# Bias rows for two attention heads computed in place, and four loads moved to another queue

## The chip, the core and the metric

The kernel runs on one core of a Trainium2 chip. A core has a matrix engine (TensorE, PE in the profile), a vector engine (VectorE, DVE), a scalar engine (ScalarE, ACT), a general engine (GpSimd, POOL) and a sequencer that issues transfers (SyncE, SP). SBUF is on-chip memory of 128 partitions; PSUM, in 8 banks, takes what TensorE produces. SP and POOL issue DMA transfers, each into a queue of its own; the profile calls SP's "hardware_dynamic" (q1) and POOL's "software_dynamic" (q0). The metric is the device time of one execution in microseconds (us), the median of several runs.

## The reference

Attention over 8 batches of 8 heads (576 positions, 64 features each), with a bias that depends on a running sum of a gate `s`, and then a gated feed-forward block over all 4608 tokens.

```python
scores = (1/8) * q @ k.T
cum    = cumsum(maximum(s, 0))
bias   = -(cum[:, None] - cum[None, :])          # minimum with 0 under the causal mask
scores = where(causal, -1e9, scores + minimum(bias, 0))
attn   = softmax(scores)
x      = (attn @ v), heads side by side          # 4608 x 512
out    = (silu(x @ w_gate) * (x @ w_val)) @ w_out
```

Inputs and output are float32.

## The kernel before

The 64 heads are worked in 16 batches of four (`hb`, 0 to 15); heads 0 and 1 of a batch lie in one half of the 128 partitions, heads 2 and 3 in the other. For a batch, k and q are loaded as float32 (`load_one`), cast to bf16 (`cast_one`, or `cast_half` for half a batch), transposed so that the features lie on partitions, and copied out of PSUM into `KQ[hb % 2][r]` (`pe_out`), r being the pair of heads: partitions 64r to 64r+63 hold the features. The other 64 partitions of the tile are zero but for the rows that carry the bias. One matmul over all 128 partitions then gives the product and the bias together.

The bias needs the running sum split into two bf16 parts, a high and a low one. `HL` holds, for each of the 64 heads, four rows for the q side and four for the k side (`HL[:, row, side, :]`, with side 0 for q): the two parts, and constants 1 and -1 that pair with them. VectorE fills it: two clears with constants (L200, L201), the scale of s (L226), the scan (L227), the high part (L230), the low part (L231) and a copy to the other side (L232). `aug(hb, engs)` (L178) then sends, per head, four rows of 2 x 576 values into the tile with one DMA; for batches 0 to 3 by SP, later by POOL.

`score_piece(bh, ci)` computes one of four chunks of a head: a mask matmul where the chunk lies on the diagonal, the score matmuls (L359), and the exponential by ScalarE (L369) straight from PSUM into `pt`. `av_piece` (L396) multiplies with V, whose rows are cast into `VT` by `cast_v` (L168) after `load_v` (L157), five pieces c = 0 to 4 of a batch; V 0 is the V of the first eight heads. The result is transposed (`x_pe`) into `XT`, and the feed-forward part (L629, L650 and following) works on 512 tokens at a time while later heads are slipped in between its steps (`attn_items`).

The order of the work is written out by hand: each engine executes its instructions in the order in which the program emits them, and the waits follow from the data. The change touches the beginning alone, up to the scores of batch 1 (heads 4 to 7). There `keep_warm(n)` puts n small matmuls whose result nobody reads on TensorE; `row_half` transposes half a batch and copies it out; `half_batch` does batch 1; `scores(h)` is the four chunks of head h. SP issues s, the four halves of k 0 and q 0, the rows of batches 0 to 3, then V 1 and k, q of batches 4 and 5. POOL issues k, q of batch 1, V 0 (five pieces), the gate weights (`w_load`, L332), and k, q of batches 2 and 3 between the casts of V 0.

Of the kernel before, what the change touches and what calls it, by code (L numbers as in the profile page):

```python
# [19 lines left out]
def kernel(  # L20
# [20 lines left out]
    HB = 4  # L41
# [56 lines left out]
    HL = const.tile([BH, 4, 2, S], BF16)  # L98
# [6 lines left out]
    s_sb = first.tile([BH, S], FP32)  # L105
    c8 = first.tile([BH, S], FP32)
# [3 lines left out]
    with tc.manual_schedule():  # L110
# [67 lines left out]
        def aug(hb, engs):  # L178
            for hh in range(HB):
# [8 lines left out]
        nc.sync.dma_start(s_sb, s.rearrange("b h n -> (b h) n"))  # L188
# [4 lines left out]
        for r in range(NR):  # L193
            load_one(0, "k", (r, r + 1))
            load_one(0, "q", (r, r + 1))

# [3 lines left out]
        nc.vector.memset(HL[:, 0:2, 0, :].bitcast(FP32), ONES2)  # L200
        nc.vector.memset(HL[:, 2:4, 1, :].bitcast(FP32), NEGS2)  # L201
# [5 lines left out]
        )  # L207

        def pads(i):
            for r in range(2):  # L210
                nc.gpsimd.memset(KQ[i][r][64 * r : 64 * r + 64, :, NR * S :], 0.0)  # L211

        for r in range(2):
            nc.gpsimd.memset(aug_rows(0, r)[:, 1, :], 0.0)
            nc.scalar.mul(
                KQ[0][r][64 * (1 - r) : 64 * (1 - r) + 64, 0, :],
                one_s[0:64, 0:1].to_broadcast([64, NR * S + 64]), 0.0,
            )
        pads(0)
        nc.vector.memset(aug_rows(1, 0), 0.0)  # L220
        for nm in ("k", "q"):
            load_one(1, nm, eng=nc.gpsimd)
        init_vt(0)
        pads(1)

        nc.vector.tensor_scalar(s_sb, s_sb, 0.0, 8.0, ALU.max, ALU.mult)  # L226
        nc.vector.tensor_tensor_scan(  # L227
            c8, one_s[0:BH, 0:1].to_broadcast([BH, S]), s_sb, 0.0, ALU.mult, ALU.add
        )
        nc.vector.tensor_copy(HL[:, 0, 1, :], c8)  # L230
        nc.vector.tensor_sub(HL[:, 1, 1, :], c8, HL[:, 0, 1, :])  # L231
        nc.vector.tensor_copy(HL[:, 2:4, 0, :], HL[:, 0:2, 1, :])  # L232
# [652 lines left out]
        def row_half(nm, r, eng):  # L885
            for g in range(2):
                pe_transpose_half(0, nm, g, r)
            for g in range(2):
                pe_out(0, nm, g, r, eng)
# [6 lines left out]
        def scores(h):  # L896
            for ci in range(4):
                score_piece(h, ci)
# [6 lines left out]
        keep_warm(32)  # L905
        cast_half(0, "k", 0, nc.scalar)
        cast_half(0, "q", 0, nc.scalar)
        aug(0, SP4)
        row_half("k", 0, nc.scalar)
        row_half("q", 0, nc.vector)  # L910
        cast_half(0, "k", 1, nc.scalar)
        cast_half(0, "q", 1, nc.gpsimd)
        nc.gpsimd.memset(aug_rows(1, 1), 0.0)
# [151 lines left out]
```

## Time and profile before

| | us |
|---|---|
| median of 3 runs | 377.03 (375.74 to 377.14) |
| profiled execution, its time | 375.79 |
| its span | 374.0 |
| TensorE busy | 360.7 (96%) |
| VectorE busy | 289.6 (77%) |
| ScalarE busy | 240.4 (64%) |
| POOL busy | 212.3 (57%) |
| first score matmul starts | 10.91 |
| first exponential starts | 11.34 |
| first feed-forward matmul starts | 25.80 |

The granted TensorE clock was 0.999 of full speed. The busy time of an engine counts its instructions alone, not the issuing of transfers by SP or POOL, which the views in order of time list as DMA_DIRECT2D with the time for which the issuing engine was held. A transfer's landing is later than its issue; for POOL's queue the profile gives the time from the one to the other. An engine that idles costs time only where the work that ends last runs through it.

### The profile page before, as it was taken

The page shows a single profiled execution, that of the slowest core. Times are in us where ns is not written, and L with a number is a line of the kernel's source. Part 1 is how long each engine was busy: PE and PEld are TensorE (multiplying, and loading weights), DVE is VectorE, ACT ScalarE, POOL GpSimd, SP SyncE. Part 2 cuts the span into 40 slices and gives each one's busy share as a digit, 9 for nine tenths or more (in the row PEclk, how much of TensorE's full clock was granted, in tenths as well). Part 3 has the DMA queues.
Part 4 walks back from the last instruction along what each step waited for, and adds up shares of the span by engine and source line. Part 5 has one row for each costly group of instructions (what it writes and reads, how often), then busy time and mean ns, then how long its engine had stood idle before and what let it go on. Part 6 is the DMA issues. An engine that isn't in the chain of part 4 may idle for free.

```text
span 374.0 us, 8759 instructions
## 1 busy us (share of the span) xinstructions
PE 360.7 (96%) x3259; PEld 230.6 (62%) x3300; DVE 289.6 (77%) x578; ACT 240.4 (64%) x471; POOL 212.3 (57%) x325
## 2 busy tenths in 40 slices
PE   7799899999999999999999999999999999999995
PEld 6584456655555556855685559655865585476464
DVE  8968776468995899588967997699858867975984
ACT  8777677698876877588757875686566523323321
POOL 8883555856455647494649464955675516315320
PEclk9999999999999999999999999999999999999999
DMA  7899999799877997896779675984132103002003
GB/s 239 193 258 253 219 257 267 237 303 247 245 186 220 254 262 196 178 281 205 211 167 266 178 182 174 255 206 98 40 119 62 35 19 128 2 0 95 20 0 114
DMA packets 97146, 64.23 MB, mean 172 GB/s; under 512 B 77232, under 2 KB 82736, under 8 KB 97104
## 3 DMA queue, kind: packets, MB, share of 16 engines
q1 hardware_dynamic: 84976, 41.46, 45.2%
q0 software_dynamic: 12128, 22.21, 22.6%
q8 instruction: 26, 0.43, 0.5%
q14 instruction: 16, 0.13, 0.1%
HBM read 37.90 MB, written 19.86 MB: 154 GB/s over the span
## 4 chain that ended last, share of the span: by engine, by line
PE 85%; DMA 6%; POOL 5%; ACT 1%; issue 1%; DVE 1%; DVEq 0%; POOLq 0%; ACTq 0%
PE bank L629 45%; PE bank L735 17%; PE bank L359 10%; PE bank L396 7%; PE bank L686 5%; DMA rawk<-in_k_dram 4%; DMA rawv<-in_v_dram 2%; POOL rawv L157 1%; POOL vt L168 1%; POOL wv L332 1%; ACT pt L369 1%; PE bank L287 0%; POOL rawq L140 0%; ACT kq L314 0%; POOL kq L211 0%
## 5 line engine op out<-in xcount | busy, mean ns | idle before, releaser
L369 ACT ACTIVATE pt<-bank 128x512 bf16<-128x512 f32 (+1 forms) x256 | 120.4, 510 | 31.0 <-PE bank L359 18.2
L629 PE MATMUL bank<-XT,wg 128*128 128x512 bf16 x418 | 110.3, 379 | 1.2 <-DVE pp L652 0.3
L629 PE MATMUL bank<-XT,wv 128*128 128x512 bf16 x412 | 109.3, 379 | 1.1
L650 ACT ACTIVATE th<-bank 128x512 bf16<-128x512 f32 x108 | 64.7, 599 | 55.9 <-PE bank L629 53.6
L652 DVE SCALAR_TENSOR_TENSOR pp<-th,bank 128x512 bf16<-128x512 bf16 x108 | 73.6, 682 | 19.2 <-ACT th L650 18.7
L663 DVE SCALAR_TENSOR_TENSOR ht<-pp,bank 128x512 bf16<-128x512 bf16 x108 | 74.1, 686 | 10.6 <-PE bank L629 0.4
L359 PE MATMUL bank<-kq 128*128 128x128 bf16 (+4 forms) x576 | 75.6, 240 | 1.5 <-DMA kq<-HL 1.0
L672 POOL TENSOR_TENSOR ht<-ht 128x512 bf16<-128x512 bf16 x35 | 40.4, 1154 | 52.2 <-DVE su L670 52.1
L359 PEld LDWEIGHTS <-kq 128*128 128x128 bf16 x576 | 45.8, 98 | 31.5 <-issue 1.9
L629 PEld LDWEIGHTS <-wv 128*128 128x128 bf16 x432 | 38.4, 98 | 36.5 <-issue 0.6
L629 PEld LDWEIGHTS <-wg 128*128 128x128 bf16 x432 | 38.3, 98 | 34.2 <-issue 0.7
L396 PEld LDWEIGHTS <-pt 128*128 128x128 bf16 x960 | 41.9, 98 | 17.2
L374 POOL TENSOR_SCALAR_AFFINE_SELECT pt<-pt 128x512 bf16<-128x512 bf16 x56 | 36.8, 658 | 27.3 <-ACT pt L369 22.7
L396 PE MATMUL bank<-vt,pt 128*128 128x65 bf16 x960 | 47.0, 194 | 0.4 <-POOL vt L168 0.3
L430 POOL DMA_DIRECT2D xs<-ot x24 | 21.7, 905 | 30.0 <-DVE ot L413 27.6
L735 PEld LDWEIGHTS <-ht 128*128 128x128 bf16 x336 | 31.2, 98 | 4.3
L413 DVE TENSOR_TENSOR ot<-bank,rc 128x320 bf16<-128x320 f32 x64 | 31.5, 492 | 2.2
L183 POOL DMA_DIRECT2D kq<-HL x48 | 28.9, 604 | 0.0
L735 PEld LDWEIGHTS <-su 128*128 128x128 bf16 x252 | 23.5, 98 | 3.3
L686 PE MATMUL bank<-wo,ht 128*128 128x512 bf16 x90 | 24.8, 379 | 0.3
L800 POOL TENSOR_TENSOR ysb<-ysb 128x512 f32<-128x512 f32 x12 | 15.2, 1270 | 15.3 <-DVE ysb L794 15.3
L379 POOL TENSOR_SCALAR_AFFINE_SELECT pt<-pt 128x64 bf16<-128x64 bf16 x56 | 14.8, 264 | 15.8 <-ACT pt L369 15.7
(93 smaller groups left out, 384.6 us busy)
## 6 DMA issues: line engine op xcount, KB each, us to landing
out_dram<-ysb POOLq DMA_DIRECT2D x32, 256.0 KB, 4.5
rawv<-in_v_dram SPq DMA_DIRECT2D x28, 256.0 KB
rawk<-in_k_dram SPq DMA_DIRECT2D x12, 576.0 KB
rawq<-in_q_dram SPq DMA_DIRECT2D x12, 576.0 KB
xs<-ot POOLq DMA_DIRECT2D x24, 160.0 KB, 3.5
ks<-ck SPq DMA_DIRECT2D x11, 288.0 KB
qs<-cq SPq DMA_DIRECT2D x11, 288.0 KB
rawk<-in_k_dram POOLq DMA_DIRECT2D x3, 576.0 KB, 7.3
```

Of the source, the lines that this page charges most:

```text
L359: nc.tensor.matmul(sc[:, o : o + w], T[:, 1, e * S + 128 * tj : e * S + 128 * (tj + 1)], T[:, 0, e * S + lo : e * S + hi], start=not maske ...
L369: nc.scalar.activation(pt[:, c0 : c0 + n], sc, AF.Exp, scale=0.125)
L374: nc.gpsimd.affine_select(pt[:, 1088:1600], pt[:, 1088:1600], pattern=[[0, 4], [1, 128]], compare_op=ALU.is_ge, fill=zreg, base=0, channel ...
L396: nc.tensor.matmul(av[:, bi * (D + 1) : (bi + 1) * (D + 1)], pt[:, c0 : c0 + 128], VT[b % 2][:, tj, h, :], start=(tj == 0), stop=(tj == bi),)
L413: nc.vector.tensor_mul(ot[:, :, e * D : (e + 1) * D], av3[:, :, 0:D], rc[:, :, None].to_broadcast([128, NCH, D]),)
L629: nc.tensor.matmul(view(bs, TT), w[:, c, f0 : f0 + 128], xt[:, c, :], start=(c == 0), stop=(c == 3),)
L650: nc.scalar.activation(th, pg, AF.Tanh, scale=0.5)
L652: nc.vector.scalar_tensor_tensor(pp, in0=th, scalar=1.0, in1=pg, op0=ALU.add, op1=ALU.mult)
L663: nc.vector.scalar_tensor_tensor(hp[:, 2 * k2 : 2 * k2 + 2, :].rearrange("p a n -> p (a n)"), in0=pp, scalar=0.5, in1=pv, op0=ALU.mult, op ...
L672: (nc.vector if ft == NFT - 1 else nc.gpsimd).tensor_sub(hp[:, 1:3, :], hp[:, 1:4:2, :], hp[:, 0:3:2, :])
L686: nc.tensor.matmul(view(pys[ts_], DM), hps[ft // 2][:, 2 * (ft % 2) + half, c0 : c0 + 128], WO[j][:, ft % WKO, :], start=(ft == 0), stop=( ...
L735: nc.tensor.matmul(ps, lhs(p), rhs(p), start=(first and p == 0), stop=(last and p == NP - 1), skip_group_check=True,)
```

## The change

It has four parts. First, heads 0 and 1 no longer get their rows by DMA. s is loaded a second time, as 32 rows (partitions 64 to 95, sixteen copies of heads 0 and 1 in turn), so the scale, scan and split run on 96 partitions instead of 64. Masks made from columns of the identity matrix (`roles`, `a_q`, `a_k`, `b_lo`) say which row is a high part, a low part or a constant, and `sums_rows(e)` writes the 32 rows of the q side and of the k side of head e into `KQ[0][0]` with two VectorE operations, four for both heads. These heads use eight rows instead of four; 32 rows of the tile are cleared again before batch 2 uses it. Second, the clears of the tiles are spread differently over ScalarE, VectorE and POOL. Third, SP issues k 1, q 1 and piece 0 of V 0, which POOL issued before. Fourth, the written order changes: the cast of the second half of k 0 goes to POOL and that of q 0 to ScalarE; batch 1's casts go from VectorE to POOL; the copies out of PSUM are dealt differently; the scores of head 0 come ahead of the transposes of the second q half; batch 1's transposes move one head later; the warming matmuls are 38, 6 and 12 instead of 32, 10 and 10.

```diff
-    HL = const.tile([BH, 4, 2, S], BF16)
+    HL = const.tile([96, 4, 2, S], BF16)
...
-    s_sb = first.tile([BH, S], FP32)
-    c8 = first.tile([BH, S], FP32)
+    s_sb = first.tile([96, S], FP32)
+    c8 = first.tile([96, S], FP32)
+    roles = first.tile([96, 4], FP32)
...
-        nc.sync.dma_start(s_sb, s.rearrange("b h n -> (b h) n"))
+        s_rows = s.rearrange("b h n -> (b h) n")
+        nc.sync.dma_start(s_sb[64:96, :], s_rows[None, 0:2, :].to_broadcast([16, 2, S]))
+        nc.sync.dma_start(s_sb[0:64, :], s_rows)
...
             load_one(0, "q", (r, r + 1))
+        load_qk(1)
...
-        nc.vector.memset(HL[:, 0:2, 0, :].bitcast(FP32), ONES2)
-        nc.vector.memset(HL[:, 2:4, 1, :].bitcast(FP32), NEGS2)
+        up = slice(64, 96)
+        for rows in (KQ[0][1][0:64, :, :], KQ[0][0][96:128, :, :]):
+            n = rows.shape[0]
+            nc.scalar.mul(
+                rows.rearrange("p a n -> p (a n)").bitcast(FP32),
+                one_s[0:n, 0:1].to_broadcast([n, NR * S + 64]), 0.0,
+            )
+        nc.vector.memset(aug_rows(1, 0), 0.0)
...
-        for r in range(2):
-            nc.gpsimd.memset(aug_rows(0, r)[:, 1, :], 0.0)
-            nc.scalar.mul(
-                KQ[0][r][64 * (1 - r) : 64 * (1 - r) + 64, 0, :],
-                one_s[0:64, 0:1].to_broadcast([64, NR * S + 64]), 0.0,
-            )
-        pads(0)
-        nc.vector.memset(aug_rows(1, 0), 0.0)
-        for nm in ("k", "q"):
-            load_one(1, nm, eng=nc.gpsimd)
         init_vt(0)
-        pads(1)
+
+        nc.vector.tensor_add(roles[up], ident[up, 64:68], ident[up, 68:72])
+        nc.vector.tensor_reduce(
+            a_q[up], roles[up, 0:2], axis=mybir.AxisListType.X, op=ALU.add, negate=True
+        )
+        nc.vector.tensor_add(a_k[up], roles[up, 2:3], roles[up, 3:4])
+        nc.vector.memset(b_lo, -1.0)
+        nc.vector.tensor_reduce(b_lo[up], ident[up, 64:68], axis=mybir.AxisListType.X, op=ALU.add)
+        nc.vector.tensor_scalar_add(b_lo[up], b_lo[up], -1.0)
+        nc.vector.memset(HL[0:64, 0:2, 0, :].bitcast(FP32), ONES2)
+        nc.vector.memset(HL[0:64, 2:4, 1, :].bitcast(FP32), NEGS2)
...
-        nc.vector.tensor_sub(HL[:, 1, 1, :], c8, HL[:, 0, 1, :])
-        nc.vector.tensor_copy(HL[:, 2:4, 0, :], HL[:, 0:2, 1, :])
+        nc.vector.scalar_tensor_tensor(
+            HL[:, 1, 1, :], in0=HL[:, 0, 1, :], scalar=b_lo, in1=c8,
+            op0=ALU.mult, op1=ALU.add,
+        )
+
+        def sums_rows(e):
+            for side, a, m in ((1, a_k, e), (0, a_q, 2 + e)):
+                nc.vector.tensor_scalar(
+                    KQ[0][0][up, side, e * S : (e + 1) * S],
+                    HL[up, 1, 1, :], a[up, :], roles[up, m : m + 1],
+                    ALU.mult, ALU.add,
+                )
...
-        keep_warm(32)
+        keep_warm(38)
         cast_half(0, "k", 0, nc.scalar)
         cast_half(0, "q", 0, nc.scalar)
-        aug(0, SP4)
-        row_half("k", 0, nc.scalar)
-        row_half("q", 0, nc.vector)
-        cast_half(0, "k", 1, nc.scalar)
-        cast_half(0, "q", 1, nc.gpsimd)
-        nc.gpsimd.memset(aug_rows(1, 1), 0.0)
-        load_v(0, range(5), nc.gpsimd)
+        load_v(0, range(1))
+        row_half("k", 0)
+        row_out("k", 0, nc.scalar, nc.scalar)
+        row_half("q", 0)
+        keep_warm(6)
+        cast_half(0, "k", 1, nc.gpsimd)
+        load_v(0, range(1, 5), nc.gpsimd)
+        sums_rows(0)
+        row_out("q", 0, nc.scalar, nc.vector)
+        row_half("k", 1)
+        cast_half(0, "q", 1, nc.scalar)
+        nc.vector.tensor_copy(HL[0:64, 2:4, 0, :], HL[0:64, 0:2, 1, :])
+        aug(0, SP4, (2, 3))
+        aug(1, SP4)
+        sums_rows(1)
         w_load("g", 0)
-        aug(1, SP4)
-        keep_warm(10)
-        row_half("k", 1, nc.scalar)
-        row_half("q", 1, nc.vector)
-        keep_warm(10)
-        cast_one(1, "k", nc.vector)
-        cast_one(1, "q", nc.vector)
+        cast_one(1, "k", nc.gpsimd)
+        cast_one(1, "q", nc.gpsimd)
+        keep_warm(12)
+        scores(0)
+        row_half("q", 1)
+        row_out("k", 1, nc.vector, nc.vector)
+        row_out("q", 1, nc.vector, nc.vector)
         for c in range(3):
             cast_v(0, c, nc.gpsimd)
         load_one(2, "k", eng=nc.gpsimd)
...
-        scores(0)
+        scores(1)
         half_batch("k")
-        scores(1)
+        score_piece(2, 0)
+        score_piece(2, 1)
         half_batch("q")
-        scores(2)
+        score_piece(2, 2)
+        score_piece(2, 3)
         scores(3)
...
         cast_v(0, 4, nc.vector)
+        nc.gpsimd.memset(KQ[0][0][up, 1, 0 : NR * S].bitcast(FP32), 0.0)
         aug(2, SP4)
```

More of the change, by code (lines that the diff above doesn't have):

```diff
@@ L104 @@
     first = first_sbuf.enter_context(tc.tile_pool(name="first", bufs=1))
-    s_sb = first.tile([BH, S], FP32)
-    c8 = first.tile([BH, S], FP32)
+    s_sb = first.tile([96, S], FP32)
+    c8 = first.tile([96, S], FP32)
+    roles = first.tile([96, 4], FP32)
+    a_q = first.tile([96, 1], FP32)
+    a_k = first.tile([96, 1], FP32)
+    b_lo = first.tile([96, 1], FP32)
     PTP = {0: first, "bufs": 7}
@@ L176, in aug_rows, with aug @@
             return KQ[i][r][r0 : r0 + 64, :, :].bitcast(FP32)
-        def aug(hb, engs):
-            for hh in range(HB):
+        def aug(hb, engs, hhs=range(HB)):
+            for hh in hhs:
                 r, e = divmod(hh, 2)
@@ L207 @@
         )
-        def pads(i):
-            for r in range(2):
-                nc.gpsimd.memset(KQ[i][r][64 * r : 64 * r + 64, :, NR * S :], 0.0)
+        nc.gpsimd.memset(aug_rows(1, 1), 0.0)
+        nc.gpsimd.memset(KQ[0][0][0:96, :, NR * S :], 0.0)
+        nc.gpsimd.memset(KQ[0][1][64:128, :, NR * S :], 0.0)
         for r in range(2):
-            nc.gpsimd.memset(aug_rows(0, r)[:, 1, :], 0.0)
-            nc.scalar.mul(
-                KQ[0][r][64 * (1 - r) : 64 * (1 - r) + 64, 0, :],
-                one_s[0:64, 0:1].to_broadcast([64, NR * S + 64]), 0.0,
-            )
@@ L219 @@
-        pads(0)
-        nc.vector.memset(aug_rows(1, 0), 0.0)
-        for nm in ("k", "q"):
-            load_one(1, nm, eng=nc.gpsimd)
-        init_vt(0)
-        pads(1)
+            nc.gpsimd.memset(KQ[1][r][64 * r : 64 * r + 64, :, NR * S :], 0.0)
+        init_vt(0)
+        nc.vector.tensor_add(roles[up], ident[up, 64:68], ident[up, 68:72])
[3 more added lines that the diff above has]
+        nc.vector.tensor_add(a_k[up], roles[up, 2:3], roles[up, 3:4])
@@ L226 @@
+        nc.vector.memset(b_lo, -1.0)
[3 more added lines that the diff above has]
+        nc.vector.memset(HL[0:64, 2:4, 1, :].bitcast(FP32), NEGS2)
         nc.vector.tensor_scalar(s_sb, s_sb, 0.0, 8.0, ALU.max, ALU.mult)
         nc.vector.tensor_tensor_scan(
-            c8, one_s[0:BH, 0:1].to_broadcast([BH, S]), s_sb, 0.0, ALU.mult, ALU.add
+            c8, one_s[0:96, 0:1].to_broadcast([96, S]), s_sb, 0.0, ALU.mult, ALU.add
@@ L883, in keep_warm, with row_half, row_out @@
                 nc.tensor.matmul(view(spare, 128), ident, ident, start=True, stop=True)
-        def row_half(nm, r, eng):
+        def row_half(nm, r):
             for g in range(2):
                 pe_transpose_half(0, nm, g, r)
+        def row_out(nm, r, *engs):
             for g in range(2):
-                pe_out(0, nm, g, r, eng)
+                pe_out(0, nm, g, r, engs[g])
         def half_batch(nm):
```

## The prediction

> **What bounds the kernel now.** I read the page first (busy times, the chain that ended last), then the first 45 us by stages and in order of time, because every edit lies in the first 20 us. The page says that from about 40 us on the kernel is TensorE work end to end:
>
> ```profile
> PE 360.7 (96%) x3259; PEld 230.6 (62%) x3300; DVE 289.6 (77%) x578; ACT 240.4 (64%) x471; POOL 212.3 (57%) x325
> ...
> PE   7799899999999999999999999999999999999995
> ...
> PE 85%; DMA 6%; POOL 5%; ACT 1%; issue 1%; DVE 1%; DVEq 0%; POOLq 0%; ACTq 0%
> ```
>
> So a microsecond gained or lost before the feed-forward part starts (25.8 us) reaches the end, except where a later stall absorbs it. What sets that start is seen in the order of time (start, length, engine, line; in brackets the idle time before it):
>
> ```profile
> 4.21 1.35 DVE L227 TENSOR_TENSOR_SCAN c<-one_s,s_sb 64x576 f32<-64x576 f32 x1
> ...
> 6.08 0.75 DVE L231 TENSOR_TENSOR HL<-c,HL 64x576 bf16<-64x576 f32 x1
> ...
> 7.51 16.73 SPq L183 DMA_DIRECT2D kq<-HL  x16
> ...
> 9.51 4.89 POOL L157 DMA_DIRECT2D rawv<-in_v_dram  x5
> ...
> 10.91 0.83 PE L359 MATMUL bank<-kq 128*128 128x128 bf16 x8 [0.99 <-DMA kq<-HL]
> ...
> 11.34 13.53 ACT L369 ACTIVATE pt<-bank 128x512 bf16<-128x512 f32 x32 [1.63 <-PE bank L359]
> ```
>
> The first scores wait for the bias rows' DMA, 3.4 us after its issue at 7.51. Then 32 exponentials run on ScalarE without a gap from 11.34 to 24.87, 0.423 us each: this stage is ScalarE's, and its end lets the feed-forward part begin. One more stall of TensorE is large, and the chain that ended last passes through it (start, length, what):
>
> ```profile
> 22.81 15.78 DMA rawk<-in_k_dram
> ...
> 38.72 1.15 POOL ck L246
> ...
> 39.92 0.45 PE bank L287 x5
> ```
>
> TensorE idles 1.16 us there until k of batch 3 has landed and been cast. In the DMA stages (busy time of each engine, granted clock, DMA share, GB/s) two holes show, where POOL's k, q 1 start late and where they have ended before V arrives:
>
> ```profile
> 6.00:7.00 1.00, 1.00 (x17) 0.86 (x16) 0.93 (x3) 1.00 (x2) 0.90 (x3) 1.00 1.04 157
> ...
> 9.00:10.00 1.00, 0.92 (x15) 0.71 (x13) 0.93 (x2) 0.71 (x2) 1.00 (x2) 1.00 0.94 383
> 10.00:11.00 1.00, 0.09 (x2) 0.10 (x3) 0.97 (x2) 0.00 (x0) 1.00 (x2) 1.00 0.24 81
> ```
>
> **Step 1, the first exponential.** VectorE, from 1.06: clear of KQ[1] 1.1; six tiny operations for the masks at 0.06 (the 128x1 clear) to 0.19 (the 128x5 reciprocal), 0.4 to 1.2, say 0.8; the two HL clears 1.2 (start to start); scale, scan, cast and low half 3.25, the scan's 96 rows costing what 64 do. That ends at 7.4, as now. The two row operations for head 0 are new: 32x576 in bf16, bounded by half of the 64x1152 copy (0.27) and by the 0.55 of the float one; 0.45 each, by the 576-wide cast at 0.45: 8.3. One q copy, 0.72: 9.0. ScalarE: one more issue on SP (0.59) stands before k 0, so its cast starts by 5.3 instead of 4.69; casts 1.3, three copies of 0.7, the first 0.55 after the k cast as now: 8.6. TensorE: the second k half, cast on POOL (0.66 after a landing near 6.9, 0.6 later than the packets show now): 7.55; it also waits for ScalarE's k copies (7.9), transposes 0.69, twelve warming matmuls at 0.073: 9.5. The last is latest, so the first exponential is at 9.5 + 0.43 = 9.9, 1.4 us earlier. The clears moved between ScalarE, POOL and VectorE lie beside the loads until 4.7 and cost nothing there; were that cover gone, 0.37 to 1.1 each.
>
> **Step 2, head 2.** Heads 0 and 1 end at 9.9 + 8 x 0.423 = 13.3. Two things must then be there; now head 2 starts its exponentials at 14.7.
> (a) The transposes of batch 1's k now stand ahead of head 2 on TensorE, and their cast moves from VectorE (0.76 and 1.12) to POOL, behind V's issues. POOL: 7.55, three issues at 1.05 and the half one at 0.69 (from the 4.89), wg 0.78, cast 1.14: 13.3. Transposes 0.67 and 0.65 to the first exponential: 14.6, level with now. The early start is spent here.
> (b) Its bias rows still come by SP's queue, and there the change puts 1.15 MB of k, q 1 and the first 256 KB of V ahead of them. SP's queue is served in order: the k load issued at 43.39 moves its first packet at 49.0, when the V pieces before it end. And V pieces on SP starve beside POOL's traffic:
>
> ```profile
> 24.54 18.74 SPq L157 DMA_DIRECT2D rawv<-in_v_dram  x5
> ```
>
> Five issues held SP 18.7 us. From 29 to 34 us the packets alternate one for one, some 190 of V's 256 bytes each and 190 of the weights' 768 bytes per us; alone, at 44 us, V made 800. The moved piece has 64 packets per DMA engine. k, q 1 end near 10.5 (7.5, and 512 packets at 173 per us). From 9.6 POOL's queue holds V's other parts (14 packets per engine, 0.2 to 0.27 us each) and from 13.5 wg 0 (32 per engine, about 0.12 us). If the two queues alternate throughout, the piece ends with wg 0, at 18.3. By the issue row (18.74 us for 4.5 such pieces, 4.2 each) it ends at 15; alone it would take 1.3 us: 12. I take 17.5, near the alternation, which is the same pair of queues at packet level, less some turns in gaps before wg 0. Rows of head 2 then land at 17.6, its exponentials start at 18.2, and the remaining 24 need 10.15: 28.4. ScalarE's stage ends 3.5 us later; both ends kept: -0.1 (a alone) and +4.3.
>
> **Step 3, behind it.** POOL casts the moved piece first of V, so k 2, q 2 and five loads behind it are issued 1 to 2.5 us later (k 3 at 24 to 25 instead of 22.81). The transfers before them are done by 18 instead of 22.9 (wg 0's issue at 14.39 plus 8.5), so k 3 lands within 1 us of now, while TensorE asks for it 3.5 us later: the 1.16 us stall goes, -1.2. In case (a) alone k 3 is ahead by 1 to 3 us and the stall goes too. Next late would be the stalls of 32 to 36 us (0.8 in all, VectorE and ScalarE pacing), which stay.
>
> [...]
>
> **Costed at nothing.** ScalarE's half cast of q (0.67) lies before the first exponential; VectorE's four more copies (1.36 moved from ScalarE, 1.46 kept) end before 14, beside heads 0 and 1, and without that cover cost 0.7 each. The eight copies for batch 1 end at about 20 instead of 18.0, when the late heads still need them no earlier. The clear of 32 rows on POOL (0.55) sits after k 3's issue, where POOL idles 1.36 us; but the SP issue for batch 2's head 0 waits for it, and behind that stand seven row issues and V 1.
>
> **Sum.** +3.5 - 1.2 = +2.3 on the profiled execution (span 374.0, time 375.79, 1.8 outside): 378.1. The median of the runs is 377.03, 1.24 above that execution, so the forecast is 379.3, slower; its own range is 377.6 (piece at 15.5) to 380.6.
>
> **Rivals.**
> A, the piece finds gaps. If it has its 64 turns before wg 0's packets begin, it lands by 14 and (a) decides: -0.1 - 1.2 = -1.3, 375.7, not slower. The point is that: V's parts leaving some 1 us of gap per engine between 10.5 and 13.5. For it: POOL's issues are 1.05 apart and four packets take 0.8 at best. Against it: V's packets now take 0.27 on average, and bias rows sent beside them land 3 to 5 us after their issue.
> B, V 1 slips as well. SP's row issues for batch 2 wait for POOL's clear, V 1 is issued near 29 instead of 24.54 and lands up to 3 us after the 49 of now; its last cast is asked for from 52.5. Price 0 to 2 over the forecast: 381.
> C, ScalarE never stalls: casts and rows of head 2 by 13. The full 1.4 and the 1.2 come: 374.4. Against it: POOL's sum in (a).
>
> **How the numbers follow.** Forecast 0.48, A 0.27, B 0.10, C 0.15. A measurement of this kernel tells about 0.5% (1.9 us) from no change. Faster: C and a little of A, 0.16. Within: most of A and the part of the forecast with the piece before 17, 0.39. Slower: the rest of the forecast and B, 0.45. The range goes from near C (374.6) to B (381.2).
>
> **What would show it.** Step 1: first exponential near 9.9. Step 2: a ScalarE gap after the eighth, ended by the DMA of the bias rows (forecast) or by the batch 1 cast (A), and none in C; V's first cast on POOL waiting for its DMA. Step 3: no TensorE wait on k 3's cast near 40 us. I am wrong if the moved piece lands by 14, or if TensorE after 30 us makes up the late start.

## The result, and the profile after

The changed kernel takes 380.40 us (median of 7 runs, 377.97 to 382.33) where the kernel before takes 375.88 (7 runs, 375.46 to 377.19): ratio 1.0111, 95% interval 1.0074 to 1.0148. It is slower by 4.2 us by that ratio and by 4.5 between the two medians; the forecast was 379.3, which was 2.3 above the 377.03 that the median of before's first three runs was. The profiled execution took 377.97 (span 376.0) against 375.79 (374.0) before, which is +2.2 where the sum of the forecast said +2.3. One thing has to be known to read the rest: executions of the changed kernel differ more than those of before, and its profiled one is the fastest of its seven, so a second trace of it was taken (below).

In order of time, the lines of the changed kernel that answer to those shown of before (start, length, engine, line; in brackets the idle time before and what ended it):

```profile
8.50 3.54 POOL L161 DMA_DIRECT2D rawv<-in_v_dram  x4
...
9.84 0.91 DVE L943 COPY HL<-HL 64x1152 bf16<-64x1152 bf16 x1
...
10.55 1.69 ACT L391 ACTIVATE pt<-bank 128x512 bf16<-128x512 f32 x4 [0.28 <-PE bank L381]
...
10.83 19.14 SPq L187 DMA_DIRECT2D kq<-HL  x14
...
11.40 1.53 DVE L250 TENSOR_SCALAR kq<-HL,a_q,roles 32x576 bf16<-32x576 bf16 x1
...
13.41 1.69 ACT L391 ACTIVATE pt<-bank 128x512 bf16<-128x512 f32 x4 [1.16 <-PE bank L381]
...
17.22 0.62 PE L381 MATMUL bank<-kq 128*128 128x128 bf16 x6 [1.00 <-DMA kq<-HL]
...
17.65 8.43 ACT L391 ACTIVATE pt<-bank 128x512 bf16<-128x512 f32 x20 [2.55 <-PE bank L381]
...
28.91 0.59 PE L651 MATMUL bank<-XT,wg 128*128 128x512 bf16 x2
```

Read it from the top. The first exponential starts at 10.55 instead of 11.34: the rows written by VectorE are worth 0.8 us. Then ScalarE stops twice, 1.16 us before head 1 and 2.55 us before head 2 (13.41 and 17.65), where it ran without a gap before. Head 1 waits because the second of its row operations (11.40) took 1.53 us, not 0.42; head 2 waits for its bias rows, which SP issued only at 10.83 and which TensorE gets at 17.2. The feed-forward part starts at 28.91 instead of 25.80, 3.1 later. One thing is given back. From 30 to 40 us TensorE is busy for 9.18 us of 10, where it was 8.02 before: the stall for k of batch 3 is gone (the kernel before, then the changed one; columns: the stretch, its us, then busy us and instructions of PE, PEld, which are the weight loads of TensorE, DVE, ACT, POOL, the granted clock, the DMA share, GB/s):

```profile
30.00:40.00 10.00, 8.02 (x50) 4.02 (x50) 8.64 (x13) 7.22 (x14) 2.93 (x5) 1.00 1.20 259
...
30.00:40.00 10.00, 9.18 (x67) 5.14 (x67) 8.26 (x13) 7.80 (x14) 1.53 (x4) 1.00 1.21 262
```

The best single view is how late each kernel is against before at the same activation of the feed-forward part (ScalarE's `th`, 108 of them; start in the trace minus start in the trace of before, in us). It shows at once which losses last and which are absorbed:

| kernel | 1st, 30 us | after the k 3 stall, 41 us | after V 1, 57 us | 120 us | 159 us | last, 360 us |
|---|---|---|---|---|---|---|
| changed kernel | +3.11 | +1.77 | +1.78 | +1.98 | +1.98 | +2.13 |
| the same, second trace (e8) | +1.26 | -0.08 | +1.72 | +2.52 | +3.88 | +4.00 |
| e1 | +1.66 | +0.33 | +0.33 | +0.33 | +0.33 | +1.40 |
| e2 | +3.47 | +2.14 | +2.15 | +2.15 | +3.51 | +3.76 |
| e3 | +2.46 | +1.12 | +4.92 | +5.33 | +6.68 | +6.85 |
| e4 | +4.72 | +3.38 | +3.38 | +3.38 | +3.39 | +3.38 |
| e5 | +2.80 | +1.47 | +3.38 | +3.38 | +3.39 | +3.41 |
| e6 | +2.96 | +1.63 | +1.64 | +1.64 | +3.01 | +3.17 |
| e7 | +3.15 | +1.82 | +1.82 | +1.82 | +3.44 | +3.47 |
| e9 | +6.75 | +5.42 | +5.41 | +5.41 | +6.75 | +6.91 |
| e10 | +1.05 | -0.29 | -0.29 | -0.28 | -0.28 | -0.28 |
| e11 | +7.68 | +6.34 | +7.18 | +7.34 | +7.34 | +7.37 |
| e12 | +1.85 | +0.69 | +0.68 | +0.67 | +0.67 | +1.74 |

Every one of them gets 1.33 us back at the k 3 stall (in e12 two small steps lie beside it). Behind it there are places where some traces lose and others don't: V 1 near 53 us, a step of 1.35 near 140 us, one of 1.07 near 298 us (e1 and e12, not followed up here), and smaller ones.

### The profile page after: what moved, and what is told of

Its sections match the earlier page's. It is cut to its first block, busy times and chain, and to the rows that moved or that the text cites. A ratio compares the mean times of both kernels' runs of the same rounds, so it can differ in the third digit from the quotient of the medians.

```text
span 376.0 us, 8775 instructions
## 1 busy us (share of the span) xinstructions
PE 361.9 (96%) x3263; PEld 231.0 (61%) x3304; DVE 293.2 (78%) x587; ACT 239.9 (64%) x470; POOL 210.8 (56%) x323
## 4 chain that ended last, share of the span: by engine, by line
PE 85%; DMA 6%; DVE 3%; issue 2%; ACT 1%; POOL 1%; SPq 1%; DVEq 0%; ACTq 0%; POOLq 0%
PE bank L651 46%; PE bank L757 17%; PE bank L381 10%; PE bank L418 7%; PE bank L708 3%; DMA XT<-xs 2%; DVE kq L338 2%; DMA kq<-HL 2%; DMA rawk<-in_k_dram 1%; DMA xs<-ot 1%; DVE pp L674 1%; ACT pt L391 1%; POOL vt L172 1%; PE bank L467 1%; PE bank L309 1%
## 5 line engine op out<-in xcount | busy, mean ns | idle before, releaser
L674 DVE SCALAR_TENSOR_TENSOR pp<-th,bank 128x512 bf16<-128x512 bf16 x108 | 73.7, 682 | 19.2 <-ACT th L672 18.6
L401 POOL TENSOR_SCALAR_AFFINE_SELECT pt<-pt 128x64 bf16<-128x64 bf16 x56 | 14.7, 262 | 17.5 <-ACT pt L391 17.3
```

What stands on the lines that cost most here:

```text
L674: nc.vector.scalar_tensor_tensor(pp, in0=th, scalar=1.0, in1=pg, op0=ALU.add, op1=ALU.mult)
```

## The experiments

The theory after the result: the rows of head 2 are late and the row operations long because VectorE and POOL hold each other up and because rows issued by SP wait while other transfers are in flight. The rivals: the moved V piece in SP's queue alone (as forecast); the later start alone; and, for the 2.4 us by which the median lies above the profiled execution, TensorE's clock.

**e1: V 0 wholly on POOL again**

```diff
-        load_v(0, range(1))
...
-        load_v(0, range(1, 5), nc.gpsimd)
+        load_v(0, range(5), nc.gpsimd)
```

> The changed kernel with piece 0 of V 0 issued by POOL again, ahead of pieces 1 to 4 (SP keeps k, q of batch 1). In the changed kernel the bias rows of head 2 are issued at 10.8 us and land at 17.2, though SP's queue had moved its last V packet at 13.3. Theory Q (the moved piece stands ahead of the rows in SP's queue): the rows land by 13, the first exponential of head 2 comes at 14.6 instead of 17.65, the feed-forward part starts near 26 and the time falls by 3 us. Theory T (rows sent while POOL's V pieces are in flight are slow, whatever SP's queue holds): nothing moves for the better, the rows land at 17 to 18.5 since POOL now moves five V pieces, and the feed-forward part starts at 28.5 to 30.

Measured: 377.35, span 375.3. With nothing of V in SP's queue the rows of head 2 still moved their first packet 2.6 us after their issue at 10.67, at 13.29. Head 2 starts at 16.07, the feed-forward part at 27.46. The piece is therefore not what makes the whole of the rows' delay. Against the one trace of the changed kernel this is 1.45 us better at the start of the feed-forward part; but its second trace started at 27.07, so a difference of this size between two single traces proves nothing about V.

**e2: the copy ahead of the row operations**

```diff
+        nc.vector.tensor_copy(HL[0:64, 2:4, 0, :], HL[0:64, 0:2, 1, :])
         sums_rows(0)
...
-        nc.vector.tensor_copy(HL[0:64, 2:4, 0, :], HL[0:64, 0:2, 1, :])
```

> The changed kernel with VectorE's copy of the bias parts to the other side of HL ahead of the two row operations of head 0, so that SP can issue the rows of heads 2 to 7 at about 8.6 us instead of 10.8; head 0's rows come 0.6 later. Theory I (late issue: the rows miss the time before POOL's V pieces arrive at 11.6): they land at 13 to 14, head 2 starts its exponentials at 14.7 to 15.5, the feed-forward part starts at 26 to 27 and the time is 1.5 to 2.5 us below the changed kernel. Theory T alone: landing is bound to the end of V's traffic, so they land at 16 to 17 again. Theory Q: they land right behind the moved piece, at 13.5.

Measured: 379.61, span 377.7. SP issued the rows at 8.98, 1.85 us earlier, and their first packet moved at 13.06, 4.07 us after. They were no longer what head 2 waited for, but head 1 was: its two row operations took 1.29 and 2.35 us (the second, from 12.00 on, beside POOL's two casts of batch 1), so head 1's exponentials started at 15.04 and head 2's at 17.90. An earlier issue alone moves the wait; and TensorE, busy for only 0.94 us of the 2 from 10 us on, then ran at half its clock for 3.4 us (0.58 granted from 12 to 14 us, 0.57 from 14 to 16):

```profile
12.00:14.00 2.00, 1.90 (x12) 1.13 (x12) 2.00 (x2) 0.94 (x3) 2.00 (x2) 0.58 1.05 225
```

**e3: POOL issues V behind its casts**

```diff
-        load_v(0, range(1, 5), nc.gpsimd)
...
         cast_one(1, "q", nc.gpsimd)
+        load_v(0, range(1, 5), nc.gpsimd)
```

> The changed kernel with POOL's issue of V pieces 1 to 4 moved behind the gate weights and the two casts of batch 1, so V's packets start about 2.5 to 3 us later (near 14) and the weights' packets come first (near 10.7). Theory T for V pieces alone: the rows of head 2, issued at 10.8, land at 13 to 13.5; head 2 starts at 14 and the feed-forward part at 26. Theory T for any traffic of POOL's queue: the weights slow them alike, landing at 15 to 17. Theory Q: no change from the changed kernel's 17.2.

Measured: 382.53, span 380.7. Head 1's row operations, which in the changed kernel took 0.69 and 1.53, are both short, and head 1's stall falls from 1.16 to 0.38. The rows of head 2 stay late (issued at 10.19, first packet at 14.45):

```profile
10.15 0.42 DVE L250 TENSOR_SCALAR kq<-HL,a_k,roles 32x576 bf16<-32x576 bf16 x1
...
10.49 0.41 DVE L250 TENSOR_SCALAR kq<-HL,a_q,roles 32x576 bf16<-32x576 bf16 x1
...
15.99 0.61 PE L381 MATMUL bank<-kq 128*128 128x128 bf16 x6 [1.81 <-DMA kq<-HL]
```

In this trace POOL issues nothing beside the copy and these operations, and they aren't stretched; the rows are late all the same, so lateness doesn't come from the stretching alone. That the shorter stall is this edit's doing isn't shown: the second trace of the unaltered changed kernel (e8) has it at 0.38 as well, amid POOL's issues. The time went elsewhere: V's parts are later, V 1 is later still, TensorE waits 2.5 us for V 1's casts between 54 and 59 us, and its clock is cut twice (0.50 granted from 18 to 20 us, 0.58 from 58 to 62).

**e4: the rows alone; k, q 1 and V 0 issued by POOL as before**

```diff
-        load_qk(1)
...
+        for nm in ("k", "q"):
+            load_one(1, nm, eng=nc.gpsimd)
...
-        load_v(0, range(1))
-        load_v(0, range(1, 5), nc.gpsimd)
+        load_v(0, range(5), nc.gpsimd)
```

> The rows by VectorE, the clears and the written order of the changed kernel, but k, q of batch 1 and all of V 0 issued by POOL as before. It parts the rows from the moved loads. Theory Q: the rows of head 2 are free of SP's queue and land by 13; then POOL's casts of batch 1 decide (two more issues ahead, about 15.5) and head 2 starts at 16.5. Theory T: the rows land at 17 to 18.5 again and head 2 starts at 18 to 19. The first exponential comes at 10 to 10.6 in either case.

Measured: 378.84, span 376.9, the feed-forward part 4.7 us later than before. The copy, with three of POOL's five V issues beside it, takes 1.74 us; the last row operation takes 2.34, beside POOL's two casts of batch 1:

```profile
9.99 1.74 DVE L943 COPY HL<-HL 64x1152 bf16<-64x1152 bf16 x1
...
12.89 1.15 POOL L269 CAST ck<-rawk 128x1152 bf16<-128x1152 f32 x1
12.96 2.34 DVE L251 TENSOR_SCALAR kq<-HL,a_q,roles 32x576 bf16<-32x576 bf16 x1
...
13.98 1.15 POOL L269 CAST cq<-rawq 128x1152 bf16<-128x1152 f32 x1
```

The first exponential is at 10.45 here too. So the rows in place bring their 0.8 us with or without the moved loads; it is the next heads that lose it.

**e5: all of V 0 by SP, behind the rows; the copy directly behind head 0's row operations**

```diff
-        load_v(0, range(1))
...
-        load_v(0, range(1, 5), nc.gpsimd)
         sums_rows(0)
+        nc.vector.tensor_copy(HL[0:64, 2:4, 0, :], HL[0:64, 0:2, 1, :])
+        aug(0, SP4, (2, 3))
+        aug(1, SP4)
+        load_v(0, range(5))
```

> The changed kernel, but all five parts of V 0 are issued by SP, behind the bias rows of heads 2 to 7, and the copy that these rows need comes directly behind the row operations of head 0; POOL issues no V. Theory (the late rows come from VectorE operations that stretch while POOL issues transfers, and from V ahead of the rows; both cost the 3.1 us at the start of the feed-forward part): the row operations take 0.42 each and the copy 0.45, the rows of head 2 are issued by 9.5 and land by 13.5, head 2's exponentials start by 14.5, ScalarE's stage ends at 24.5 to 25.5 and the feed-forward part starts near 26. With the stall at k 3 gone the time is 373.5 to 375.5, below both kernels. Rival (it is the number of transfers in flight, whoever issues them and in whatever order): the rows land after 15.5, head 2 starts after 16 and the time is 377 or more. Second rival: V 0 comes too late for the first products with V, and the feed-forward part starts after 28.

Measured: 380.61 (6 runs, 378.92 to 381.69), ratio 1.0123, 1.0085 to 1.0162. Head 1's stall is 0.38, as the theory had it, though one of its row operations still took 1.24 us, beside POOL's cast of k 1 (10.40 to 11.60). The rows were issued at 9.59, as it had it too, but TensorE got head 2's at 15.65:

```profile
9.59 4.37 SPq L187 DMA_DIRECT2D kq<-HL  x6
...
15.65 0.61 PE L381 MATMUL bank<-kq 128*128 128x128 bf16 x6 [0.61 <-DMA kq<-HL]
```

SP's queue had moved its last k, q packet by 11.45 and then moved nothing until 14.15, while the packets of POOL's first gate weights ran alone. The first rival was right, more than the theory: without any V ahead of them the rows were 4.56 us from issue to first packet, the first 1.9 of them while k, q 1 still moved. And V 1, whose issue by SP stands behind the rows of batch 2, came so late that TensorE stalled for it, 1.2 us at 56.07 and 0.8 us beside it, which is the forecast's rival B.

**e6: more warming matmuls in the two gaps**

```diff
+        keep_warm(8)
         scores(1)
         half_batch("k")
+        keep_warm(16)
```

> The changed kernel with 8 more warming matmuls ahead of the scores of head 1 and 16 more ahead of those of head 2, in the two places where TensorE waits. Theory (the runs of the changed kernel lie up to 4 us above its profiled one because TensorE's clock is cut after the thin stretches at 10 to 17 us): granted clock .999 or more, the median within 0.5 us of 378 and the runs close together; the start of the feed-forward part stays at 28.5 to 29.2. Rival (the spread has another cause, or more matmuls draw the clock down later): median 380 and a spread of 4 us as in the changed kernel, or a clock under .996 in spite of the added matmuls.

Measured: 379.89 (6 runs, 379.02 to 382.15), ratio 1.0103, 1.0065 to 1.0141. The clock was 0.998 or more in five of the six runs, where five of the changed kernel's seven had 0.996 or less; that half of the theory holds. The time did not follow: the median is 0.5 below the changed kernel's, with intervals that overlap, and runs at a clock of 0.998 took 379.6 to 382.2. So the clock is one part of the spread and not the whole.

**e7: the moved loads alone, in the kernel before**

```diff
             load_one(0, "q", (r, r + 1))
+        load_qk(1)
...
-        for nm in ("k", "q"):
-            load_one(1, nm, eng=nc.gpsimd)
...
+        load_v(0, range(1))
         aug(0, SP4)
...
-        load_v(0, range(5), nc.gpsimd)
+        load_v(0, range(1, 5), nc.gpsimd)
```

> The kernel before with one part of the change alone: k, q of batch 1 and the first part of V 0 are issued by SP ahead of the bias rows; rows, clears and order are those of before, so all bias rows still come by DMA, issued near 7.5 to 8.5. Queue theory (rows wait behind the moved loads in SP's queue): the rows of head 0 land at 12.5 to 14 instead of 10.5, the first exponential starts at 13 to 14.5 instead of 11.34, the feed-forward part starts 2 to 3 us later than 25.80 and the time is 377 to 379. Rival (loads ahead cost the rows nothing, it was VectorE's late issue alone): first exponential at 11.3 to 11.8 and the time 374.5 to 376.

Measured: 379.13, span 377.3.

```profile
7.47 19.92 SPq L183 DMA_DIRECT2D kq<-HL  x16
...
12.75 1.39 PE L358 MATMUL bank<-kq 128*128 128x128 bf16 x8 [1.53 <-DMA kq<-HL]
13.31 1.69 ACT L368 ACTIVATE pt<-bank 128x512 bf16<-128x512 f32 x4 [3.34 <-PE bank L358]
...
28.96 0.59 PE L628 MATMUL bank<-XT,wg 128*128 128x512 bf16 x2
```

The numbers come close to what the queue theory said; the time lies 0.1 over its range. The rows of head 0 are issued at 7.47 as before. Their first packet moves 3.25 us later, at 10.72, where it took 2.17 in before, and their last by 11.03, while k, q 1 (until 11.31) and the V piece (until 12.22) still move. TensorE is released at 12.75, 1.7 us after that last packet, where it was 0.9 in before. Whether that second wait comes from the V piece isn't shown: in the first trace of the changed kernel the packets of head 2's rows had moved by 15.6 and TensorE was released at 17.22, 1.6 later, with V's last packet on SP gone by 13.03. The first exponential is 2.0 us later and the feed-forward part 3.2. In this trace, moving the loads ahead of rows that go by DMA costs the start of the feed-forward part as much as the whole change did in its first trace.

**e8: the changed kernel once more**

> The changed kernel once more, unaltered, for a second trace: its profiled execution of before, 377.97, lies 2.4 below its median. Theory (a late start costs twice: TensorE is thin from 10 to 18 us, after which its clock is cut to half for 3.4 us in most executions, and VectorE and POOL meet in another phase later): about 380, with one stretch of 3.4 us at a granted clock of .5 before 22 us, or a step of 0.8 to 1.4 us near 140 us, where a VectorE operation on bf16 lasts as long as the POOL operations beside it. Rival (executions differ from the start on, by when the first loads land): clock 1.0, no step later, and the whole difference already there at the first feed-forward matmul, which then starts at 30.5 to 31.5 instead of 28.91.

Measured: 379.92, span 377.9, clock 1.0 throughout. In order of time:

```profile
8.78 3.61 POOL L161 DMA_DIRECT2D rawv<-in_v_dram  x4
...
9.78 0.45 DVE L943 COPY HL<-HL 64x1152 bf16<-64x1152 bf16 x1
...
10.26 0.62 DVE L250 TENSOR_SCALAR kq<-HL,a_k,roles 32x576 bf16<-32x576 bf16 x1
...
10.81 0.41 DVE L250 TENSOR_SCALAR kq<-HL,a_q,roles 32x576 bf16<-32x576 bf16 x1
10.83 1.69 ACT L391 ACTIVATE pt<-bank 128x512 bf16<-128x512 f32 x4 [0.65 <-PE bank L381]
...
15.80 8.48 ACT L391 ACTIVATE pt<-bank 128x512 bf16<-128x512 f32 x20 [1.21 <-PE bank L381]
...
27.07 0.59 PE L651 MATMUL bank<-XT,wg 128*128 128x512 bf16 x2
...
54.50 0.62 POOL L172 CAST vt<-rawv 128x512 bf16<-128x512 f32 x1 [1.53 <-DMA rawv<-in_v_dram]
55.17 0.19 PE L418 MATMUL bank<-vt,pt 128*128 128x65 bf16 x1 [1.87 <-POOL vt L172]
...
142.10 0.65 POOL L396 TENSOR_SCALAR_AFFINE_SELECT pt<-pt 128x512 bf16<-128x512 bf16 x1
142.13 1.89 DVE L693 TENSOR_TENSOR su<-ht 128x256 bf16<-128x256 bf16 x1
142.70 1.16 POOL L694 TENSOR_TENSOR ht<-ht 128x512 bf16<-128x512 bf16 x1
```

The same program started its feed-forward part 1.84 us earlier than in its first trace (27.07) and still ended 1.87 later. The copy and head 1's row operations took 0.45, 0.62 and 0.41 us where the first trace has 0.91, 0.69 and 1.53, with POOL issuing V beside them in both; head 1 waits 0.38 instead of 1.16, and the first packet of head 2's rows moves 2.8 us after its issue instead of 4.0. So the size of both losses changes from one execution of the program to the next. What it gained at the start it lost at 55.17, where TensorE waited 1.87 us for V 1 (in the first trace the same cast ran at 54.76 without a wait; its later start left V 1 time to land, and behind this place both traces stand at +1.7 to +1.8). Then it lost 0.8 between 103 and 122 us (0.65 of it a wait for a transposing transfer at 121.73) and 1.35 near 142. There a VectorE operation of 0.28 us took 1.89: POOL's selection had started 0.03 us ahead of it, and VectorE's operation ended at 144.02, after POOL's next one (142.70 to 143.86) too. In the first trace the two meet almost as closely, POOL's start recorded 0.02 us ahead; there VectorE's operation takes its 0.28, and it is POOL's selection that takes longer, 0.79 instead of 0.65:

```profile
141.57 0.79 POOL L396 TENSOR_SCALAR_AFFINE_SELECT pt<-pt 128x512 bf16<-128x512 bf16 x1
141.59 0.28 DVE L693 TENSOR_TENSOR su<-ht 128x256 bf16<-128x256 bf16 x1
```

The same operation takes 1.89 to 1.90 in e2, e3, e6, e7, e8 and e9, and 0.28 in before, in the first trace of the changed kernel and in e1, e4, e5, e10, e11 and e12. The rival (everything decided at the start) falls. The theory had two candidates for the loss; the clock was not one in this execution, the step near 140 us was, and the largest, V 1, it had not named. Later steps like that of 1.35, and the clock cuts of other executions, are thus ways in which the median comes to lie above the profiled execution; how often each comes in the runs without a trace is open.

**e9: the row operations in VectorE's three-operand form**

```diff
-                nc.vector.tensor_scalar(
+                nc.vector.scalar_tensor_tensor(
                     KQ[0][0][up, side, e * S : (e + 1) * S],
-                    HL[up, 1, 1, :], a[up, :], roles[up, m : m + 1],
-                    ALU.mult, ALU.add,
+                    in0=HL[up, 1, 1, :], scalar=a[up, :],
+                    in1=roles[up, m : m + 1].to_broadcast([32, S]),
+                    op0=ALU.mult, op1=ALU.add,
                 )
```

> The changed kernel with the four row operations of heads 0 and 1 written in VectorE's three-operand form, which the trace shows at 0.67 to 0.81 for 512 to 576 columns whatever POOL does, in place of the two-operand form that took 0.80, 0.42, 0.69 and 1.53. Theory (the two-operand bf16 form has to wait while POOL holds something that both use, the three-operand form has not): each of the four takes 0.65 to 0.80 with POOL issuing V or casting beside it; only the copy between the halves of the split still stretches. The first exponential starts up to 0.3 later or earlier, head 1's stall falls from 1.16 to under 0.8. Rival (the stretching is VectorE waiting for SBUF in general, or for the profile's bookkeeping): at least one of the four takes over 1.2.

Measured: 382.75, span 380.8. The theory was wrong on the form: the four took 1.10, 0.80, 1.65 and 3.74 us. The last one began while POOL issued the gate weights and ended at 16.29, when POOL's two casts of batch 1 were over and its three casts of V under way:

```profile
12.11 0.78 POOL L355 DMA_DIRECT2D wg<-in_moe_w_gate_dram  x1
12.55 3.74 DVE L250 SCALAR_TENSOR_TENSOR kq<-HL,a_q,roles 32x576 bf16<-32x576 bf16 x1
...
12.87 1.17 POOL L269 CAST ck<-rawk 128x1152 bf16<-128x1152 f32 x1
13.96 1.17 POOL L269 CAST cq<-rawq 128x1152 bf16<-128x1152 f32 x1
...
15.05 2.48 POOL L172 CAST vt<-rawv 128x512 bf16<-128x512 f32 x3
```

The three-operand form alone thus doesn't keep an operation short. L674 has the same form and stays at 0.66 to 0.69 us in all its 108 executions in the changed kernel's first trace, the 66 that ran beside an operation of POOL's among them. It reads one input from PSUM, where these four read both from SBUF; whether that is the reason was not varied. As near 142 us, the long operation here outlasted POOL's first one beside it: its 3.74 us span two casts and reach into the next row of three. While POOL did nothing but issue V, from 8.34 to 12.80 in e1, a row operation took 1.56 us, so one can be long beside issuing alone; in e8, beside the same issuing, the two took 0.62 and 0.41.

**e10: the kernel before, with k of batch 3 issued ahead of the second weights**

```diff
+        load_one(3, "k", eng=nc.gpsimd)
         for nm in ("g", "v"):
             w_load(nm, 1, 0)
-        load_one(3, "k", eng=nc.gpsimd)
```

> The kernel before with one line moved: k of batch 3 is issued by POOL ahead of the second group of gate and value weights instead of behind it. Nothing of the change is in it. Theory (the only gain in the changed kernel was that TensorE asked for k of batch 3 later, so that its stall of 1.16 went; the same gain is to be had without the late start): the feed-forward part starts at 25.8 as before, the stall near 40 us is under 0.3, and the time is 1.0 to 1.4 below that of before, 374.4 to 374.9, faster than both kernels. Rival (the weights that are now later are themselves late): a new wait of TensorE for weights between 28 and 38 us, time 375.5 to 377.

Measured: 375.81 (12 runs, 375.16 to 377.83) against 375.57 for before (17 runs, 374.73 to 376.79): ratio 1.0013, 0.9996 to 1.0031. In the trace the stall is gone, and no new wait stands for it (POOL's cast of k 3 with no idle time before it):

```profile
38.20 1.14 POOL L246 CAST ck<-rawk 128x1152 bf16<-128x1152 f32 x1
```

But this execution had started its feed-forward part 1.05 us later than the trace of before, because VectorE's cast of k 1 began at 11.81, after a wait for its load, instead of 10.56; the moved line is reached only at 21.3. So the one trace ends 0.28 ahead, and the median shows no gain at all: the theory's 1.0 to 1.4 is refuted as a gain, and why the removed stall doesn't show in the median is open. The table suggests a reading, which is argued and not shown: the stall is a reserve of 1.33 us that late executions of before use up, so taking it away helps only the early ones.

**e11: e5 with POOL's first gate weights behind its casts**

```diff
-        w_load("g", 0)
         cast_one(1, "k", nc.gpsimd)
         cast_one(1, "q", nc.gpsimd)
+        w_load("g", 0)
```

> The kernel with all of V 0 issued by SP behind the rows, and in addition POOL's first gate weights issued behind its two casts for batch 1, about 4 us later. There the rows of head 2 were issued at 9.59 and moved their first packet at 14.15 while only weight packets ran. Theory (the weight packets in flight delay the rows): without them the first row packet moves within 2.5 us of its issue, at 11.5 to 12.2, and head 2's exponentials start at 14.3 to 15.2 instead of 16.08. Rival (the delay from issue to first packet has nothing to do with POOL's packets): still 4 us or more, head 2 at 15.7 or later.

Measured: 382.86, span 381.0.

```profile
9.54 4.26 SPq L187 DMA_DIRECT2D kq<-HL  x6
...
12.90 8.41 ACT L391 ACTIVATE pt<-bank 128x512 bf16<-128x512 f32 x20 [0.38 <-PE bank L381]
...
21.96 0.22 PE L418 MATMUL bank<-vt,pt 128*128 128x65 bf16 x2 [2.05 <-POOL vt L172]
...
28.10 1.09 ACT L391 ACTIVATE pt<-bank 128x512 bf16<-128x512 f32 x2 [6.79 <-PE bank L381]
```

On the rows the theory is confirmed: with no weight packets in flight the six rows' first packets move 1.25 to 1.44 us after their issues, where e5's took 2.7 to 4.6, and ScalarE runs 20 exponentials without a gap from 12.90. This is the state that the forecast's rival C described. The price came next: V, issued by SP at 13.85 beside the weights, held SP for 8.4 us, TensorE waited for V 0 from 20 us on, and ScalarE stood for 6.8 us before head 6. Why a row waits so long beside weights is open. One estimate can be made from this trace: from 16.8 to 18.5 us V's packets of 256 bytes on SP's queue and the weights' of 1536 bytes on POOL's pass in equal number, some 56 of each per half microsecond, and 99% of V's are followed by another 0.142 us later, which is the 0.134 of one weight packet and a little more. If a row took its turn like these, it would wait about 0.14 us, and not the 2.7 to 4.6 measured in e5.

**e12: what the runs pointed to, together**

```diff
         sums_rows(0)
+        nc.vector.tensor_copy(HL[0:64, 2:4, 0, :], HL[0:64, 0:2, 1, :])
+        aug(0, SP4, (2, 3))
+        aug(1, SP4)
...
-        cast_half(0, "q", 1, nc.scalar)
+        cast_half(0, "q", 1, nc.gpsimd)
+        load_v(0, range(2), nc.gpsimd)
         sums_rows(1)
         cast_one(1, "k", nc.gpsimd)
         cast_one(1, "q", nc.gpsimd)
+        load_v(0, range(2, 5), nc.gpsimd)
+        w_load("g", 0)
...
+        scores(1)
+        nc.gpsimd.memset(KQ[0][0][up, 1, 0 : NR * S].bitcast(FP32), 0.0)
         for c in range(3):
             cast_v(0, c, nc.gpsimd)
...
+        load_one(3, "k", eng=nc.gpsimd)
         for nm in ("g", "v"):
             w_load(nm, 1, 0)
```

(the same calls no longer stand at their old places, and SP issues no piece of V 0)

> What the runs point to, in one kernel: the rows of heads 0 and 1 by VectorE; the copy and SP's row issues directly behind the first row operations, with no V and no weights in flight before them; V 0 all on POOL, two parts issued while POOL waits for k of batch 1 and three behind its casts; the gate weights, the clear of the 32 rows (ahead of the V casts, so that SP's rows for batch 2 and V 1 are issued early) and k of batch 3 ahead of the second weights behind these. Theory (late rows, the late clear and the late k of batch 3 were what the change paid): rows of head 2 moving within 2 us of their issue, ScalarE's 32 exponentials with gaps under 1.5 us in all, feed-forward part from 25.2 to 26.3, V 1 issued by 25.5, no step near 53 us, stall near 40 us under 0.6: 374.0 to 375.5, below both kernels. Rival (V 0 now comes too late, since its last parts and everything behind them on POOL are 3 us later than before): a wait of the products with V at 20 to 24 us, feed-forward part after 27, time 376.5 or more. Second rival (row operations of head 1 stretch beside POOL's two V issues): head 1 starts after 13.2 and the time is 375.5 to 376.5.

Measured: 378.73 (6 runs, 377.69 to 379.40) against 375.50 (11 runs): ratio 1.0081, 1.0053 to 1.0108.

```profile
9.67 16.32 SPq L187 DMA_DIRECT2D kq<-HL  x14
...
14.87 6.82 ACT L391 ACTIVATE pt<-bank 128x512 bf16<-128x512 f32 x16 [0.40 <-PE bank L381]
...
21.75 0.81 PE L418 MATMUL bank<-vt,pt 128*128 128x65 bf16 x21 [1.11 <-POOL vt L172]
...
27.55 0.59 PE L651 MATMUL bank<-XT,wg 128*128 128x512 bf16 x2
```

The rows move 1.3 to 2.1 us after their issue, ScalarE's gaps before heads 1 and 2 are 0.38 and 0.40, and V 1 is issued in time: no step near 53 us. But the first rival happened: POOL comes to V's casts at 18.57 instead of 15.16, TensorE waits 1.11 us for one at 21.75, and the feed-forward part starts at 27.55. No version here beats the kernel before.

## Why the prediction was right, and where it was not

**Right in part by luck.** The direction held, and the sum fits the profiled execution, +2.3 for +2.2. But that execution is the fastest of seven, the second trace has +1.26 at the first activation and +4.00 at the last, and one of the sum's main terms, step 2(b), came out with a mechanism that the packets refute. The level of 379.3 came near 380.40 because two misses cancel in part: the median of before that it was built on, 377.03 from three runs, is 375.88 over seven, and the change itself, forecast at 2.3, is 4.2 to 4.5. Its own range doesn't follow from its sum either: the piece at 15.5 gives 377.3 and not 377.6, the later end of +4.3 gives 380.1 and not 380.6.

**The bound.** That a microsecond before the feed-forward part reaches the end, less what a later stall absorbs, held in the first trace: +3.11 there, -1.33 at k 3, +2.13 at the last activation and +2.0 in the span. In the second it didn't: +1.26 became +4.00, by steps behind 50 us.

**Step 1** forecast the first exponential at 9.9; it came at 10.55, and at 10.83 in the second trace. The term that failed is POOL's half cast of k, put at an end of 7.55: it waited 2.28 us for its load, began at 7.89 and ended at 8.55. Behind it the transposes start at 8.61, not near 7.55. Of the 1.4 us that the step counted, 0.8 came, and 0.5 in the second trace.

**Step 2(a)** put POOL's cast of k 1 at an end of 13.3; it ended at 13.95 in the first trace and 14.3 in the second, for the same reason. In the second trace it is what head 2 waits for longest (TensorE 1.01 us, and then 0.2 for the rows), before its exponentials start at 15.80.

**Step 2(b)** is the one whose mechanism failed while its size came out. It had the moved V piece end in SP's queue at 17.5, one for one with POOL's packets, and rows landing at 17.6 behind it. The packets show the piece moving from 10.43 to 13.03: POOL's own V packets began only at 11.34 (its issues stood behind the late cast), so the piece found the gaps that rival A asked for, and it was done before 14, which is the sign of being wrong that the prediction had set itself. The rows landed at 17.2 all the same, by two things that the step did not have. Their issue came at 10.83, because the copy they need stood behind the row operations and itself took 0.91; and from issue to first packet they took 4.0 us, with POOL's transfers in flight (2.8 in the second trace). e5 shows 4.56 without any V ahead of them, e11 shows 1.44 once POOL's packets are gone. What the prediction itself held against rival A, bias rows landing 3 to 5 us after their issue, was the term to use, for (b) and not only against A. And the 1.16 us stall before head 1, which is 0.38 in the second trace, was not in the sum: it priced the row operations at 0.45 each as if VectorE were alone. ScalarE's stage ended 3.1 us later, with 3.5 forecast.

**Step 3** forecast -1.2 at k 3 and got -1.33. The reason given first, transfers done earlier, isn't needed: e4, with the loads on POOL as before, loses the stall as well, since TensorE asks later.

**Costed at nothing, and rival B.** The clear of 32 rows on POOL was named as what SP's issues for batch 2 wait for. V 1 was issued at 30.20 instead of 24.54. In the first trace that costs nothing, in the second 1.8 us, in e5 1.9. Rival B, at 0.10, thus came in one of the changed kernel's two traces; in e1, e2 and e6, with V 1 issued at 28.99 to 30.05, it did not.

**From the profile to the median.** The forecast added 1.24 us, the distance of before's median of three runs from its profiled execution. Over seven runs that distance is 0.09, so the term was an accident of few runs; for the changed kernel it is 2.43. In the forecast's sum this term, 1.24 for 2.43, is what separates 379.3 from 380.4. What replaced it is seen in part in e8 (the 0.8 between 103 and 122 us and the 1.35 near 142 us; its wait for V 1 only used up the earlier start) and is in part the clock: it was 0.996 or lower in five of seven runs, and in the traces of e2, e3, e4, e7, e9 and e11 TensorE runs at half speed for 3.41 or 6.83 us after a stretch of 3.41 in which it is busy for 18 to 55% of the time. The changed kernel's three executions at a clock of 1.0 took 377.97, 379.92 and 380.31, so the clock isn't all of it. The cases are shown; how the 2.43 divides among them is open.

## What to carry to other kernels

Before VectorE gets work at a place where POOL issues transfers or casts, price its operations at up to several times their own length (0.42 us became up to 2.35 here). A small transfer that something waits for should be issued before bulk transfers of any queue are in flight, not only ahead of them in its own (its first packet moved 1.25 to 1.44 us after its issue in e11, 2.7 to 4.6 beside the weights in e5). And one trace of a start-up phase is worth no more than about 2 us here (the feed-forward part started at 28.91 in one trace and at 27.07 in another of the same program): take a second of the same program before two variants are compared.

## What the runs showed of the hardware

- The same VectorE operation near 142 us took 1.89 to 1.90 us in six traces (with POOL's selection recorded 0.03 us ahead of it in e7 and e8) and 0.28 in the first trace of the changed kernel with POOL 0.02 ahead, where POOL's selection took 0.79 instead of 0.65.
- Row operations of 0.42 us took up to 2.35 beside POOL's casts (e2, e4) and up to 1.56 beside its issuing of transfers alone (e1); beside the same issuing they took 0.41 and 0.62 in e8. L674's operations, which have an input in PSUM, kept to 0.66 to 0.69 (changed kernel, 108 of them, 66 beside an operation of POOL's).
- A row transfer of SP moves its first packet 1.25 to 1.44 us after its issue with no POOL packets in flight (e11), 1.3 to 2.7 in before up to 13.2 us, and 2.7 to 4.6 beside weights alone (e5); the rows of batch 2, issued from 24.3 us on in the changed kernel, take 4.0 to 4.2, one like the other.
- From the last packet of a row transfer to the release of TensorE it took 0.9 us in before, 1.6 in the first trace of the changed kernel and 1.7 in e7; what sets it isn't shown.
- In the traces of e2, e3, e4, e7, e9 and e11 the granted clock was cut to one half seven times (0.50 from 16 to 18 us in e4, for one), five times for 3.41 us and in e9 and e11 for 6.83. In the 3.41 us before each of the seven TensorE was busy for 18 to 55%; 55% also went uncut, from 14.66 in the changed kernel's first trace.
